# Attention then mixture of experts: one more head turns its score tiles by VectorE and DRAM instead of on TensorE

## The chip, the cores and the metric

The kernel runs on one core of a Trainium2 chip. The metric is the device time of one execution in microseconds. A change of up to 0.3% (2.3 us) is about what a measurement of this kernel cannot tell from no change.

## The reference

There are two stages. The first is attention with a hash mask over 2 batches of 8 heads, 768 tokens and 64 dimensions. The second is a layer of 4 experts on the attention's output. Cut to what matters:

```python
q_bucket, k_bucket = hash6(q @ proj), hash6(k @ proj)      # 6 sign bits
scores = where(q_bucket == k_bucket, q @ k.T / 8, -1e9)
attn = softmax(scores) ; x = attn @ v                      # per batch and head
x = x.transpose -> (1536, 512) ; p = domain_probs / sum
out = sum_e p[:, e] * (relu(x @ w1[e]) @ w2[e])            # w1 512x1024, w2 1024x512
```

All arithmetic has float32 accuracy. The kernel gets it from float32r matmuls, in which each operand is split into a high part and a low part (`...hi`, `...lo`).

## The kernel before

Attention goes through 96 score tiles of 128 queries by 768 keys. There are six tiles to a head, and two neighbouring tiles make a group g, so a head has three groups. A step `i` issues one stage of several tiles. The letters of `ORDER = "THXVSEYNRP"` say which stages stand in a step and in which order. A stage with a lag works on tile `i - lag`. So the row of instructions on each engine is written out by hand, and every engine takes its row strictly in order.

- S (`stage_s`, L344 to L351): TensorE makes the scores of a tile, VectorE takes them out to a tile `p`. E (L367): ScalarE takes the exponential, one step later.
- The `p` tiles must then be turned so that keys lie on partitions. **A heavy head** does this in T (`stage_t`, lag 6): six TensorE transposes of 128x128 (L407), then ScalarE copies them to `pthi` (L411) and VectorE subtracts for `ptlo` (L412).
- **A light head** does it by group. In X (lag 3) VectorE makes two 32x32 block transposes of 128x768 (L426) into `t1`, and SyncE writes `t1` to DRAM (`scr`, L430, 768 KB). In Y (lag 4) SyncE reads it back in four DMAs (L439) into `ptlo`. In H (lag 6) ScalarE copies it in two pieces to `pthi` (L452), and GpSimd subtracts in two pieces (L453).
- V (`stage_v`, L463, lags 7 and 8): TensorE multiplies with the values, first with `pthi`, a step later with `ptlo`. ScalarE and VectorE take out the result (L483, L488 or L495). After an odd head of batch 0 GpSimd scales it and splits it (L497, L501, L504) into the tiles `xs`, the input of the experts.
- P prepares the next head: transposes of q and k (L260), ScalarE (L264) and VectorE (L265), then L276, L278, L284 and five small copies by DMA (L268 to L270, L277, L292).

`LIGHT_FROM` is the number of the first light head (heads are numbered through both batches, 8 is the first head of batch 1).

Up to about 150 us attention of batch 0 runs alone. Then the experts' layer of batch 0 (`moe`) runs on TensorE. Each of 8 units `u` has 8 chunks of 12 matmuls (L683 to L685) with a relu by ScalarE (L690) and a split by VectorE (L691), and then 6 chunks of the second layer (L646 to L648, L652). Attention of batch 1 is put between the chunks: before the next attention stage is issued, a sum of nominal stage costs is compared with the sum of the chunks' costs:

```python
n_att = sum(1306 + 654 * (not light(b, h)) for b, h, t in seq if b) + H * 1632 + LAG_VL * DRAIN
while da < dm * ATT_PACE * n_att / n_moe:   # dm: chunks issued, da: attention issued
```

The last part, the experts' layer of batch 1 (`moe_fast`), starts when all attention is over.

All DMAs are issued from SyncE's queue, also in a fixed order. The experts' weights come in halves of 512 KB (`ws`, L604) into two buffers. VectorE copies one to `w...hi` (L622), GpSimd subtracts for `w...lo` (L615), and only after that is the buffer free for the next `ws`. `PSUM` results use six slots in turn: two large ones, and four small ones that the chunks, T and V share.

In this text tile 48 is the first tile of the first head of batch 1, and its groups are g0 (tiles 48 and 49), g1 and g2. S(54) is the stage S of tile 54.

Of the kernel before, what the change touches and what calls it, by code (L numbers as in the profile page):

```python
# [35 lines left out]
W_STEP = 12  # L36
PREP_AT = 0
ORDER = "THXVSEYNRP"
LIGHT_FROM = 9
LAG_VL = 7  # L40
DRAIN = 1000
LAG_X = 3
# [5 lines left out]
def tile_lsh_attention__then__domain_moe(  # L48
# [276 lines left out]
    def light(b, h):  # L325
        return b * H + h >= LIGHT_FROM

# [634 lines left out]
```

## Time and profile before

| | |
|---|---|
| time, median of 3 runs (lowest, highest) | 753.21 us (751.62, 753.64) |
| span of the profiled execution, first to last instruction | 749.5 us |
| TensorE busy | 733.6 us, 98% of the span |
| VectorE, ScalarE, GpSimd busy | 69%, 48%, 46% |
| TensorE's share of the chain that ended last | 82% |
| TensorE's time in L407 (324 transposes) | 45.8 us as the sum of their lengths |

How to read it: the time of the profiled execution is not listed apart from its span. The median of the runs lies 3.7 us above that span, so that much is taken to lie around it. Matmuls overlap in a pipeline, so what one costs TensorE is the distance between starts, not its listed length. The granted clock of TensorE is a share of 2.4 GHz, 0.5 being the lower level of 1.2 GHz.

### The profile page before, as it was taken

Reading aid. Unit: us, or ns where it says so; the run is one execution under the profiler, and the core shown is the slowest. Engines: PE = TensorE matmul, PEld = TensorE weight load, DVE = VectorE, ACT = ScalarE, POOL = GpSimd, SP = SyncE. Lnnn points to the kernel's source line nnn. Section 1 sums busy time; section 2 is a strip of 40 time slices with the busy share of each in tenths; the row PEclk is TensorE's granted clock in tenths of the full one; section 3 lists DMA queues with packets and bytes.
Section 4 is the critical chain, followed back from the end, with each engine's and each line's share of the span. In section 5 each row is a group of like instructions: output and inputs, shape, how many; then the busy total and the mean of one; then the engine's idle time right before and its main releaser. Section 6 shows DMA issues by size and latency. Waiting matters only on the chain.

```text
span 749.5 us, 11443 instructions
## 1 busy us (share of the span) xinstructions
PE 733.6 (98%) x4090; PEld 668.7 (89%) x4090; DVE 517.3 (69%) x957; ACT 363.2 (48%) x731; POOL 342.7 (46%) x290
## 2 busy tenths in 40 slices
PE   7899999999999999999999999999999999999997
PEld 6798899898998999989999899888988989889896
DVE  4899999856568756686676543887558575675752
ACT  4999999843353544534635210443425234253330
POOL 1233525422466656584857653854334243343430
PEclk9999999999999999999999999999999999999999
DMA  3554454341877697878677511152121221212202
GB/s 99 126 145 102 114 145 122 98 126 61 233 210 195 197 261 224 209 204 247 180 228 225 156 57 57 56 169 85 35 78 57 80 90 30 83 57 68 101 1 84
DMA packets 71953, 95.49 MB, mean 127 GB/s; under 512 B 31396, under 2 KB 47268, under 8 KB 71896
## 3 DMA queue, kind: packets, MB, share of 16 engines
q1 hardware_dynamic: 71896, 94.76, 44.3%
q8 instruction: 32, 0.52, 0.3%
q14 instruction: 25, 0.20, 0.1%
HBM read 62.68 MB, written 19.71 MB: 110 GB/s over the span
## 4 chain that ended last, share of the span: by engine, by line
PE 82%; DVE 8%; ACT 3%; POOL 3%; DMA 2%; issue 1%; SPq 0%; POOLq 0%; DVEq 0%; ACTq 0%
PE mps L646 11%; PE mps L648 11%; PE mps L647 11%; PE mps L683 6%; PE mps L685 6%; PE mps L684 6%; PE pv L463 6%; PE sps L346 3%; PE sps L344 2%; PE mps L841 2%; PE mps L837 2%; PE mps L840 2%; DVE p L351 2%; PE hps L276 2%; PE pa L840 2%; PE pa L837 1%
## 5 line engine op out<-in xcount | busy, mean ns | idle before, releaser
L646 PE MATMUL mps<-w2hi,hh 128*128 128x512 f32 x384 | 151.6, 395 | 0.8 <-DVE acc L654 0.4
L648 PE MATMUL mps<-w2hi,hl 128*128 128x512 f32 x384 | 151.0, 393 | 0.0
L647 PE MATMUL mps<-w2lo,hh 128*128 128x512 f32 x384 | 150.0, 391 | 0.0
L453 POOL TENSOR_TENSOR ptlo<-ptlo,pthi 128x768 fp32r<-128x768 f32 x42 | 78.1, 1880 | 70.1 <-ACT pthi L452 56.1
L654 DVE SCALAR_TENSOR_TENSOR acc<-mps,pe,acc 128x512 f32<-128x512 f32 x84 | 62.7, 747 | 62.0 <-PE mps L648 60.9
L690 ACT ACTIVATE hh<-mps 128x384 fp32r<-128x384 f32 x64 | 31.4, 491 | 139.4 <-PE mps L685 139.2
L823 POOL TENSOR_TENSOR w2lo<-ws,w2hi 128x512 fp32r<-128x512 f32 x32 | 45.9, 1453 | 113.9 <-ACT w2hi L822 113.9
L367 ACT ACTIVATE p<-p,nb 128x768 f32<-128x768 f32 x96 | 89.6, 933 | 11.5 <-DVE p L351 10.7
L351 DVE TENSOR_SCALAR_CACHE_REDUCE p<-sps 128x768 f32<-128x768 f32 x96 | 90.6, 945 | 5.2 <-PE sps L346 4.9
L646 PEld LDWEIGHTS mps<-w2hi,hh 128*128 128x128 f32 x384 | 72.1, 188 | 17.8 <-ACT hh L851 2.8
L648 PEld LDWEIGHTS mps<-w2hi,hl 128*128 128x128 f32 x384 | 72.1, 188 | 17.5 <-DVE hl L852 2.4
L683 PE MATMUL mps<-xs,w1hi 128*128 128x384 f32 x256 | 86.7, 338 | 0.5 <-DVE hl L691 0.5
L685 PE MATMUL mps<-xs,w1lo 128*128 128x384 f32 x256 | 86.2, 337 | 0.0
L684 PE MATMUL mps<-xs,w1hi 128*128 128x384 f32 x256 | 86.0, 336 | 0.0
L647 PEld LDWEIGHTS mps<-w2lo,hh 128*128 128x128 f32 x384 | 72.3, 188 | 13.2
L691 DVE SCALAR_TENSOR_TENSOR hl<-mps,hh 128x384 fp32r<-128x384 f32 x64 | 35.5, 555 | 55.6 <-ACT hh L690 55.0
L615 POOL TENSOR_TENSOR w1lo<-ws,w1hi 128x512 fp32r<-128x512 f32 x32 | 42.0, 1319 | 40.0 <-DVE w1hi L622 38.3
L412 DVE TENSOR_TENSOR ptlo<-ptps,pthi 128x384 fp32r<-128x384 f32 x108 | 54.5, 546 | 7.5 <-ACT pthi L411 7.3
L346 PE MATMUL sps<-k,al 76*128 76x384 f32 x192 | 50.5, 343 | 3.3 <-POOL vv L305 1.7
L344 PE MATMUL sps<-ah,q 128*128 128x384 f32 x192 | 50.6, 344 | 1.9 <-DVE ah L244 1.1
L782 POOL TENSOR_TENSOR w1lo<-ws,w1hi 128x512 fp32r<-128x512 f32 x24 | 35.9, 1496 | 34.0 <-ACT w1hi L778 34.0
L615 POOL TENSOR_TENSOR w2lo<-ws,w2hi 128x512 fp32r<-128x512 f32 x32 | 41.8, 1313 | 20.7 <-issue 6.6
(134 smaller groups left out, 1576.6 us busy)
## 6 DMA issues: line engine op xcount, KB each, us to landing
ws<-in_moe_w_dram SPq DMA_DIRECT2D x64, 512.0 KB
scr<-t SPq DMA_DIRECT2D x21, 768.0 KB
ptlo<-scr SPq DMA_DIRECT2D x84, 192.0 KB
q<-ah SPq DMA_DIRECT2D x30, 192.0 KB
tv<-in_v_dram SPq DMA_DIRECT2D x16, 192.0 KB
rdb<-row SPq DMA_DIRECT2D x48, 64.0 KB
out_dram<-acc SPq DMA_DIRECT2D x12, 256.0 KB
tqk<-in_q_dram SPq DMA_DIRECT2D x15, 192.0 KB
```

Source lines behind the costliest of these rows:

```text
L344: nc.tensor.matmul(ps[:, i, :NH], q1[:, sl], k1[:, i * NH : (i + 1) * NH], start=True, stop=False)
L346: nc.tensor.matmul(ps[:, i, :NH], q2[0:MQE, sl], k2[0:MQE, i * NH : (i + 1) * NH], start=False, stop=True)
L351: nc.vector.tensor_scalar(out=two(pt), in0=ps[:, :, :NH], scalar1=MASKED, scalar2=MASKED, op0=ALU.min, op1=ALU.min, accum_out=nb,)
L367: nc.scalar.activation(pt, pt, ACTF.Exp, bias=nb, scale=-1.0, accum_out=dens[b, h, g][:, o : o + 1])
L453: nc.gpsimd.tensor_tensor(out=fl[:, sl], in0=px[:, sl], in1=fh[:, sl].bitcast(F32), op=ALU.subtract)
L615: nc.gpsimd.tensor_tensor(out=lo[:, c - 1], in0=st[c - 1], in1=hi[:, c - 1].bitcast(F32), op=ALU.subtract)
L646: nc.tensor.matmul(ps, hh[:, ts], w2hi[:, f], start=f == 0, stop=False)
L647: nc.tensor.matmul(ps, hh[:, ts], w2lo[:, f], start=False, stop=False)
L648: nc.tensor.matmul(ps, hl[:, ts], w2hi[:, f], start=False, stop=f == FC - 1)
L683: nc.tensor.matmul(ps[:, :SB], w1hi[:, kk, fs], xhi[b, kk][:, sl], start=kk == 0, stop=False)
L684: nc.tensor.matmul(ps[:, :SB], w1hi[:, kk, fs], xlo[b, kk][:, sl], start=False, stop=False)
L685: nc.tensor.matmul(ps[:, :SB], w1lo[:, kk, fs], xhi[b, kk][:, sl], start=False, stop=kk == KD - 1)
```

## The change

One number changes. Head 8, the first of batch 1, becomes a light head, so its six tiles go through X, Y and H instead of T.

```diff
--- before.py
+++ after.py
@@ -36,7 +36,7 @@
 W_STEP = 12
 PREP_AT = 0
 ORDER = "THXVSEYNRP"
-LIGHT_FROM = 9
+LIGHT_FROM = 8
 LAG_VL = 7
 DRAIN = 1000
 LAG_X = 3
```

`light(b, h)` is `b * H + h >= LIGHT_FROM`. The sum `n_att` falls from 86668 to 82744, and the six costs of 654 that T had returned are no longer counted. Since every stage has a lag of its own, the rows of all engines change from step 52 on. Three places:

ScalarE, where attention of batch 0 ends and the first chunks of the experts begin (the first L690). Before:

```order
L264 ACTIVATE ah<-tps,qk_scale 128x768
L411 ACTIVATE pthi<-ptps 128x3x128 x2
L483 ACTIVATE xtmp<-pv 64x256
L690 ACTIVATE hh<-mps 128x384
L367 ACTIVATE p,den<-p,nb 128x768
L278 ACTIVATE k_2378<-hps,sgn_bias 44x768
L690 ACTIVATE hh<-mps 128x384 x2
```

ScalarE at the same place, now:

```order
L264 ACTIVATE ah<-tps,qk_scale 128x768
L452 ACTIVATE pthi<-ptlo 128x768 x2
L483 ACTIVATE xtmp<-pv 64x256
L690 ACTIVATE hh<-mps 128x384
L367 ACTIVATE p,den<-p,nb 128x768
L278 ACTIVATE k_2380<-hps,sgn_bias 44x768
L690 ACTIVATE hh<-mps 128x384 x4
L367 ACTIVATE p,den<-p,nb 128x768
L370 ACTIVATE den<-den,eps 128x2
L452 ACTIVATE pthi<-ptlo 128x768 x2
```

The two copies of g0, which wait for its four DMAs, now stand ahead of the first relu of the experts; those of g1 stand behind the fifth relu.

GpSimd at the same place (`xs_120` is the last of the four input tiles of the experts, `ws` the second half of `w2` of unit 0). Before:

```order
L504 TENSOR_TENSOR xs_120<-xf,xs_120 128x256
L615 TENSOR_TENSOR w2lo<-ws,w2hi 128x512
L497 TENSOR_TENSOR xf<-xf,rdb 128x256
L501 TENSOR_SCALAR xs_120<-xf 128x256
L504 TENSOR_TENSOR xs_120<-xf,xs_120 128x256
L615 TENSOR_TENSOR w2lo<-ws,w2hi 128x512
```

GpSimd now:

```order
L504 TENSOR_TENSOR xs_120<-xf,xs_120 128x256
L453 TENSOR_TENSOR ptlo<-ptlo,pthi 128x768 x2
L497 TENSOR_TENSOR xf<-xf,rdb 128x256
L501 TENSOR_SCALAR xs_120<-xf 128x256
L504 TENSOR_TENSOR xs_120<-xf,xs_120 128x256
L615 TENSOR_TENSOR w2lo<-ws,w2hi 128x512 x2
L453 TENSOR_TENSOR ptlo<-ptlo,pthi 128x768 x2
```

Both L615 that read the weights' buffer now stand behind the subtractions of g0.

SyncE's queue from the last small copy of head 8 on (`k_2127`). Before:

```order
L292 DMA k_2127<-al 12x768
L383 DMA row<-rt 4x32 x2
L190 DMA tv<-in_v_dram 128x384
L390 DMA rdb<-row 64x256
L383 DMA row<-rt 4x32 x2
L268 DMA q_2375<-ah 64x768
L269 DMA q_2375<-ah 64x768
L270 DMA k_2378<-ah 64x768
L604 DMA ws<-in_moe_w_dram 128x2x512 x2
L390 DMA rdb<-row 64x256
```

SyncE's queue now, from the write of g0 that stands behind the same `k_2127`:

```order
L430 DMA scr<-t_2275 128x1536
L383 DMA row<-rt 4x32 x2
L190 DMA tv<-in_v_dram 128x384
L439 DMA ptlo<-scr 32x4x384 x4
L390 DMA rdb<-row 64x256
L430 DMA scr<-t_2349 128x1536
L383 DMA row<-rt 4x32 x2
L268 DMA q_2377<-ah 64x768
L269 DMA q_2377<-ah 64x768
L270 DMA k_2380<-ah 64x768
L604 DMA ws<-in_moe_w_dram 128x2x512 x2
L439 DMA ptlo<-scr 32x4x384 x4
```

The four DMAs that read g1 back stand behind the two `ws`. The second of these needs the buffer that the two L615 read. On TensorE the first L463 of g0 stood behind four chunks and one T; it now stands behind three chunks, and the first L463 of g1 behind six.

## Rows read from the trace of the kernel before

**Rows 1.** Windows: window, its length, each engine's busy us (count), PEclk, DMA share, GB/s.
```profile
200.00:250.00 50.00, 50.00 (x282) 46.97 (x282) 31.36 (x58) 23.25 (x44) 26.74 (x21) 1.00 0.81 225
```

**Rows 2.** Timeline of TensorE: start us, length, engine, line, tiles, [idle before <-releaser].
```profile
142.54 0.55 PE L407 MATMUL ptps<-ident,p 128*128 128x128 f32 x3 [0.37 <-DVE ptlo L412]
...
147.67 0.59 PE L346 MATMUL sps<-k,al 76*128 76x384 f32 x2 [1.24 <-POOL xf L497]
...
150.13 0.34 PE L683 MATMUL mps<-xs,w1hi 128*128 128x384 f32 x1
...
152.21 0.51 PE L344 MATMUL sps<-ah,q 128*128 128x384 f32 x2
...
153.97 0.33 PE L683 MATMUL mps<-xs,w1hi 128*128 128x384 f32 x1
...
158.13 0.82 PE L407 MATMUL ptps<-ident,p 128*128 128x128 f32 x6
...
158.71 0.42 PE L683 MATMUL mps<-xs,w1hi 128*128 128x384 f32 x1
...
160.90 0.88 PE L463 MATMUL pv<-pthi,vv 128*128 128x256 f32 x6
...
162.32 0.34 PE L683 MATMUL mps<-xs,w1hi 128*128 128x384 f32 x1
...
164.44 0.82 PE L407 MATMUL ptps<-ident,p 128*128 128x128 f32 x6
...
165.77 0.44 PE L683 MATMUL mps<-xs,w1hi 128*128 128x384 f32 x1 [0.52 <-DVE hl L691]
...
181.18 0.82 PE L407 MATMUL ptps<-ident,p 128*128 128x128 f32 x6
...
182.19 0.50 PE L646 MATMUL mps<-w2hi,hh 128*128 128x512 f32 x1 [0.19 <-DVE acc L652]
```

**Rows 3.** Timeline of VectorE, the first of the existing transposes.
```profile
178.22 1.83 DVE L426 STREAM_TRANSPOSE t<-p 128x768 f32<-128x768 f32 x2
```

**Rows 4.** Timeline of SyncE's queue: start us, length of issuing, line, tiles, count.
```profile
145.21 0.78 SPq L292 DMA_DIRECT2D k<-al  x1
...
180.07 0.35 SPq L430 DMA_DIRECT2D scr<-t  x1
...
212.32 0.39 SPq L604 DMA_DIRECT2D ws<-in_moe_w_dram  x1
...
272.89 2.86 SPq L439 DMA_DIRECT2D ptlo<-scr  x4
...
367.37 1.80 SPq L439 DMA_DIRECT2D ptlo<-scr  x4
```

**Rows 5.** Windows of half a microsecond, columns as in the first group.
```profile
182.50:183.00 0.50, 0.50 (x4) 0.38 (x3) 0.47 (x3) 0.08 (x1) 0.46 (x1) 1.00 0.51 197
...
218.50:219.00 0.50, 0.50 (x5) 0.50 (x4) 0.50 (x2) 0.00 (x0) 0.42 (x2) 1.00 0.22 41
```

**Rows 6.** Timeline of ScalarE, three of the 21 existing groups' copies.
```profile
195.03 1.57 ACT L452 ACTIVATE pthi<-ptlo 128x768 fp32r<-128x768 f32 x2
...
280.69 1.58 ACT L452 ACTIVATE pthi<-ptlo 128x768 fp32r<-128x768 f32 x2 [2.71 <-DMA ptlo<-scr]
...
372.78 1.58 ACT L452 ACTIVATE pthi<-ptlo 128x768 fp32r<-128x768 f32 x2 [1.00 <-DMA ptlo<-scr]
```

**Rows 7.** Timeline of GpSimd.
```profile
152.78 0.74 POOL L497 TENSOR_TENSOR xf<-xf,rdb 128x256 f32<-128x256 f32 x1 [2.67 <-DVE xf L495]
...
154.79 1.28 POOL L615 TENSOR_TENSOR w2lo<-ws,w2hi 128x512 fp32r<-128x512 f32 x1
...
195.95 3.66 POOL L453 TENSOR_TENSOR ptlo<-ptlo,pthi 128x768 fp32r<-128x768 f32 x2 [4.08 <-ACT pthi L452]
```

**Rows 8.** Windows early in the span, columns as in the first group.
```profile
14.00:18.00 4.00, 3.53 (x11) 3.15 (x12) 1.36 (x4) 1.49 (x4) 0.00 (x0) 0.57 0.59 148
...
22.00:23.00 1.00, 0.00 (x0) 0.00 (x0) 0.41 (x3) 0.98 (x5) 0.63 (x1) 1.00 0.21 37
```

## The prediction

> **What bounds the kernel now.** I read the page's busy shares first, then the windows by stage. Then TensorE is busy all the time: in the stretch from 200 to 250 us it works 50.00 of 50 us at the full clock, while VectorE, ScalarE and GpSimd work half of it or a little more and the DMA engines 0.81 [rows 1]. So a TensorE instruction taken out there is worth its distance to the next start, and nothing given to another engine costs anything until TensorE waits for it. The first thing to see in the timeline of TensorE is that the change lies in two different stretches. Ahead of 150 us attention runs alone and S(54) waits until 147.67; behind 150.13 the experts' chunks run [rows 2]. The row of that wait names GpSimd's L497, but what L346 reads is `k2`, whose last piece the small copy of L292 brings, issued at 145.21 [rows 4].
>
> **What goes.** Six T. The T of tiles 48 and 49 lie ahead of 150 us. The first is hidden by S(54), which goes on at 147.67 with it or without it; the second I count at nothing, because VectorE is later there (below). The T of tiles 50 to 53 lie between chunks: 0.58 us from 158.13 to 158.71; 1.33 from 164.44 to 165.77, with a wait of 0.52 for VectorE behind it; 0.58 for tile 52 like the first; 1.01 from 181.18 to 182.19, with a wait of 0.19 [rows 2]. Sum: **3.5 us less**. ScalarE and VectorE lose their copies and subtractions of these tiles; they bound nothing here.
>
> **What comes.** For each of three groups: two VectorE transposes, 1.83 us together [rows 3], a write of 768 KB, four reads, two ScalarE copies of 1.57 together [rows 6], two GpSimd subtractions of 3.66 together [rows 7]. The 21 existing groups do the same, and TensorE stays full. But their copies wait for DMA beside work that has slack; the first groups of head 8 come where the engines pass from attention to the experts, and the rows of instructions show what stands behind them. So I walk along them.
>
> Write of g0. The buffer `t1` that it takes holds tiles 46 and 47, so VectorE waits for the T of tile 47, over at 142.54 + 0.55 = 143.1 [rows 2], and is done at 144.9 by the 1.83. SyncE is busy with the small copy ahead of it until 145.21 + 0.78 = 146.0 [rows 4], and issues the write then. The small copy goes first, so S(54) still starts its second half at 147.67. I take 150.1 for the first chunk as before; bounds are 0.58 earlier (the T that is gone) and 1.8 later (if all VectorE transposes were on the path).
>
> Reads of g0. The first existing write was issued at 180.07, and its traffic ended in the window from 182.50, half busy, so at 182.8 [rows 4, 5]. With 0.3 us to be noticed, an estimate, that is 3.0 us from issue to landing; the reads are issued at 149.0. Four reads took 5.4 us from issue to the copy that waited for them (367.37 to 372.78), at worst 7.8 (272.89 to 280.69, with other copies around) [rows 4, 6]. I take 5.4, since the queue is nearly empty here: ScalarE's copies of g0 start at 154.4. Until then ScalarE stands still, and behind it wait the taking out of the last V of batch 0 and all relus. That alone costs TensorE nothing: it has three chunks to do first.
>
> The second half of `w1`. It takes the buffer that both L615 read. They stand behind the subtractions of g0 and the last three L497 to L504. From the start of the copies: 0.92 until GpSimd starts (195.03 to 195.95), 3.66, 2.01 (152.78 to 154.79), and twice 1.28 [rows 6, 7], 9.15 in all. So SyncE issues this load at 163.6; before, the second L615 was over at 154.79 + 1.28 = 156.1 [rows 7]. SyncE is in order, and **behind the load stand the four reads of g1**, whose own write had landed long ago.
>
> Reads of g1. A load of 512 KB and four reads behind it in a quiet queue were issued from 212.32 on, and their traffic ended at about 218.7 [rows 4, 5], 6.4 us; the copy notices some half a microsecond later (estimate from the above), and two head loads now follow in the queue, so I take 7.0 (6.4 to 8.3, the latter 0.5 for the load's issue and the 7.8). The copies of g1 start at 170.6 and end at 172.2.
>
> TensorE needs both copies for the first V of g1, which stands behind six chunks (2.08 each, 150.13 to 152.21), three S, two V and one L276: 1.76 for S and L276 (152.21 to 153.97), twice 1.42 for V and S (160.90 to 162.32) [rows 2]. 150.1 + 12.5 + 1.8 + 2.8 = 167.2. So **TensorE waits 5.0 us**, with nothing else to do since it is in order too. The third group has time: its write follows at about 171, its reads land some 8.4 us (3.0 + 5.4) behind that, and its first V stands four chunks, two S and two V later.
>
> The clock. The only low clock of the trace stands early: 0.57 on average over the 4 us from 14 us on, after a stretch with waits, which cost (1 - 0.57) x 4 = 1.7 us of full speed; but a window of 1 us without any matmul passed at the full clock [rows 8]. Five microseconds of nothing are nearer to the first, so I add **1.7**; the other bound is 0. The Trainium skill ("TensorE: Matmul & The Clock Gate", section "HAM oscillation — how this bites in real kernels") tells of waits for DMA that send the array back to its lower clock each time. By that rule the 1.7 is to be paid; by the row of 22 us alone nothing, and the sum would be 1.7 lower. No wait of this trace is long enough to show which.
>
> **Sum**: -3.5 + 5.0 + 1.7 = +3.2 us. Made on the profiled execution (749.5 span, 3.7 around it by the median), it goes onto the median: 753.2 + 3.2 = **756.4 us**. Bounds: -0.6 (6.4 instead of 7.0) and -1.7 (no lower clock) give 754.1, and the earlier start of 0.58 does not help, since the wait then grows by as much. Upwards 2.4 (7.8 for the reads of g0) and 1.3 (8.3 for those of g1) give 760.1.
>
> **The rivals.**
> The clock holds. All else as above: +1.5, 754.7, no change that can be measured. For it speaks the window without matmuls at 22 us, against it that the wait is five times as long.
>
> The DMAs are faster, and TensorE does not wait: faster than before. The two round trips lie in a queue with little else. If the reads ran at the write's pace, 2.1 us or so instead of 4, both trips would save about 4 us, the wait would shrink to 1.0, too short to move the clock, and the time would be 753.2 - 2.5 = 750.7. It decides once the copies of g1 land 3.8 us sooner than I worked out (then 1.2 of wait against 3.5). Against it: the reads of 367.37 and those behind the load of 212.32 had little beside them either, and took their 5.4 and 6.4.
>
> The DMAs are slower, as in the rows of 272.89: the upper bound, 760.1. Then the first V of g0 waits too. For it: the write of g1 is issued while the reads of g0 still run.
>
> Waits later on: the attention stages of batch 1 stand at other places beside the chunks, and the pace is 4.5% lower by `n_att`. ScalarE's wait for reads of up to 2.71 in the rows shown stayed without a wait of TensorE; I count nothing.
>
> **How the numbers follow.** The walk with both terms: 0.46, 755.5 to 758.5. Clock holds: 0.25, 754 to 755.4. DMAs faster: 0.12, 749.7 to 751. Slower, or a wait more: 0.17, 758.5 to 762. The range of 8 in 10 reaches from 750.6 to 759.9 and leaves out about half of the last case and of the faster one. Slower by over 0.3% (above 755.5) are the first and the last case and little of the second: 0.60. Within 0.3%: 0.28. Faster: 0.12.
>
> **What would show it.** In the new profile: the first two L452 at about 154.4, with ScalarE idle for some 3 us ahead of them; the load behind them issued at about 163.6, at once after the second L615; a wait of TensorE of about 5 us before an L463 near 167, released by ScalarE's L452; a window behind it with a granted clock near 0.5; no wait of TensorE over a microsecond from there to the end of attention; and four T fewer between chunks. The prediction is wrong if the reads of g1 are issued well before 163, if TensorE has work there that I did not see, or if later waits outweigh this one.

## The result, and the profile after

The changed kernel takes 756.66 us (median of 4 runs, 755.20 to 757.16), the kernel before 752.63 beside it: 1.0055 times as long, interval 1.0042 to 1.0067, so 4.0 us slower. A second comparison gave 756.44 against 751.85, 1.0064 (1.0052 to 1.0077). The prediction was 756.4, slower.

The waits of TensorE in the profile after (total, count, longest) begin with one that is new; the longest of all others is 1.4 us:

```profile
PE pv L463 <- ACT pthi L452: 5.5, 1, 5.5
```

The timeline of TensorE around it (before: [rows 2]), with S(54), L260, the first chunk, S(55), the first V of g0 and both V of g1:

```profile
146.68 0.59 PE L344 MATMUL sps<-ah,q 128*128 128x384 f32 x2 [0.69 <-issue]
148.44 0.98 PE L346 MATMUL sps<-k,al 76*128 76x384 f32 x2 [1.17 <-DMA k<-al]
149.32 1.54 PE L260 MATMUL tps<-ident,tqk 128*128 128x128 f32 x6
...
151.85 0.34 PE L683 MATMUL mps<-xs,w1hi 128*128 128x384 f32 x1
...
153.94 0.51 PE L344 MATMUL sps<-ah,q 128*128 128x384 f32 x2
...
159.86 0.88 PE L463 MATMUL pv<-pthi,vv 128*128 128x256 f32 x6
...
174.67 1.65 PE L463 MATMUL pv<-pthi,vv 128*128 128x256 f32 x6 [5.46 <-ACT pthi L452]
...
182.37 0.88 PE L463 MATMUL pv<-ptlo,vv 128*128 128x256 f32 x6
```

The first V of g0 waits for nothing; the first V of g1 waits 5.46 us, from 169.21 on. To see why, read SyncE's queue, GpSimd and ScalarE in turn [rows 4, 7, 6]:

```profile
146.88 0.46 SPq L430 DMA_DIRECT2D scr<-t  x1
...
150.31 1.76 SPq L439 DMA_DIRECT2D ptlo<-scr  x4
...
152.72 0.58 SPq L430 DMA_DIRECT2D scr<-t  x1
...
157.36 8.36 SPq L604 DMA_DIRECT2D ws<-in_moe_w_dram  x2
165.82 1.84 SPq L439 DMA_DIRECT2D ptlo<-scr  x4
```

```profile
156.96 3.83 POOL L453 TENSOR_TENSOR ptlo<-ptlo,pthi 128x768 fp32r<-128x768 f32 x2 [6.58 <-ACT pthi L452]
160.75 0.74 POOL L497 TENSOR_TENSOR xf<-xf,rdb 128x256 f32<-128x256 f32 x1
...
162.76 2.54 POOL L615 TENSOR_TENSOR w2lo<-ws,w2hi 128x512 fp32r<-128x512 f32 x2
```

```profile
156.03 1.58 ACT L452 ACTIVATE pthi<-ptlo 128x768 fp32r<-128x768 f32 x2 [4.23 <-DMA ptlo<-scr]
...
173.04 1.58 ACT L452 ACTIVATE pthi<-ptlo 128x768 fp32r<-128x768 f32 x2 [5.46 <-DMA ptlo<-scr]
```

The two issues of `ws` span 8.36 us together, although one takes 0.39 elsewhere [rows 4]. The second goes out when the second L615 is over, at 162.76 + 2.54 = 165.3. The four reads of g1 stand right behind, at 165.82, while their write had been issued at 152.72. The copies of g1 start at 173.04, and V starts as they end.

The granted clock is the column ahead of the last two in the windows:

```profile
146.00:148.00 2.00, 0.59 (x2) 0.30 (x2) 1.93 (x7) 1.03 (x2) 1.53 (x2) 1.00 0.22 65
148.00:149.00 1.00, 0.56 (x2) 0.50 (x2) 0.97 (x2) 0.00 (x0) 0.66 (x1) 0.66 0.95 399
149.00:150.00 1.00, 1.00 (x5) 0.68 (x4) 0.97 (x3) 0.70 (x1) 0.83 (x3) 0.50 0.76 296
150.00:151.00 1.00, 1.00 (x7) 1.00 (x6) 1.00 (x2) 0.73 (x4) 0.38 (x1) 0.50 0.61 143
...
170.00:172.00 2.00, 0.00 (x0) 0.00 (x0) 0.00 (x0) 0.00 (x0) 0.00 (x0) 1.00 1.11 228
172.00:174.00 2.00, 0.00 (x0) 0.00 (x0) 0.00 (x0) 0.96 (x2) 0.04 (x1) 0.55 1.26 206
174.00:176.00 2.00, 1.33 (x6) 1.33 (x7) 0.94 (x2) 1.95 (x4) 2.00 (x2) 0.50 1.15 373
176.00:178.00 2.00, 2.00 (x8) 2.00 (x8) 2.00 (x5) 0.45 (x2) 1.89 (x2) 0.50 0.17 69
178.00:180.00 2.00, 2.00 (x10) 2.00 (x10) 0.56 (x1) 0.25 (x1) 1.83 (x3) 0.74 0.92 227
```

It is low twice: behind the wait, as forecast, and already from 148 on, which the prediction did not see.

A second trace of the same kernel, taken for experiment 7, shows S(55), the wait and both V of g1 at:

```profile
154.04 0.51 PE L344 MATMUL sps<-ah,q 128*128 128x384 f32 x2
...
174.06 1.65 PE L463 MATMUL pv<-pthi,vv 128*128 128x256 f32 x6 [4.76 <-ACT pthi L452]
...
182.35 0.88 PE L463 MATMUL pv<-ptlo,vv 128*128 128x256 f32 x6
```

**A measure without the start.** The program's first 140 us vary: S(53), which no edit but `W_STEP` moves, starts at 143.64 in the trace of before and between 143.99 and 145.75 in the others, mostly by waits in the first 60 us. So I also give, for each trace, the stretch from the start of S(53) to the end of the span. The time of a run is 1.7 to 1.8 us above its span.

| kernel | S(53) | span | from S(53) on | against before |
|---|---|---|---|---|
| before | 143.64 | 749.5 | 605.86 | |
| after, two traces | 144.40, 143.99 | 755.0, 755.0 | 610.60, 611.01 | +4.7, +5.2 |
| reads ahead, two traces | 145.75, 144.65 | 749.5, 748.3 | 603.75, 603.65 | -2.1, -2.2 |
| wait filled | 144.74 | 753.5 | 608.76 | +2.9 |
| 148 filled | 144.61 | 755.7 | 611.09 | +5.2 |
| weights early | 145.12 | 749.3 | 604.18 | -1.7 |
| reads ahead and 148 filled, two traces | 144.27, 144.83 | 747.2, 748.3 | 602.93, 603.47 | -2.9, -2.4 |
| before with W_STEP = 10 | 145.68 | 750.5 | 604.82 | -1.0 |
| last group alone | 144.94 | 749.2 | 604.26 | -1.6 |

### The profile page after: what moved, and what is told of

The parts are those of the page before. It is cut to its first block, busy times and chain, and to the rows that moved or that the text cites. A ratio compares the mean times of both kernels' runs of the same rounds, so it can differ in the third digit from the quotient of the medians.

```text
span 755.0 us, 11408 instructions
## 1 busy us (share of the span) xinstructions
PE 733.9 (97%) x4054; PEld 668.1 (88%) x4054; DVE 521.7 (69%) x951; ACT 364.0 (48%) x725; POOL 352.9 (47%) x296
## 4 chain that ended last, share of the span: by engine, by line
PE 81%; DVE 10%; DMA 4%; POOL 3%; issue 1%; ACT 1%; SPq 1%; POOLq 0%; DVEq 0%; ACTq 0%
PE mps L646 11%; PE mps L648 11%; PE mps L647 11%; PE pv L463 6%; PE mps L683 5%; PE mps L685 5%; PE mps L684 5%; DVE p L351 3%; PE sps L346 3%; PE sps L344 3%; PE mps L841 2%; PE mps L837 2%; PE mps L840 2%; PE hps L276 2%; PE ptps L407 2%; DVE ptlo L412 2%
## 5 line engine op out<-in xcount | busy, mean ns | idle before, releaser
L453 POOL TENSOR_TENSOR ptlo<-ptlo,pthi 128x768 fp32r<-128x768 f32 x48 | 89.2, 1880 | 77.5 <-ACT pthi L452 70.3
L690 ACT ACTIVATE hh<-mps 128x384 fp32r<-128x384 f32 x64 | 31.3, 491 | 119.4 <-PE mps L685 119.2
L615 POOL TENSOR_TENSOR w2lo<-ws,w2hi 128x512 fp32r<-128x512 f32 x32 | 41.9, 1317 | 31.5 <-DVE w2hi L622 23.2
L412 DVE TENSOR_TENSOR ptlo<-ptps,pthi 128x384 fp32r<-128x384 f32 x96 | 48.4, 545 | 6.0 <-ACT pthi L411 5.8
L452 ACT ACTIVATE pthi<-ptlo 128x768 fp32r<-128x768 f32 x48 | 37.8, 836 | 30.5 <-DMA ptlo<-scr 30.4
L615 POOL TENSOR_TENSOR w1lo<-ws,w1hi 128x512 fp32r<-128x512 f32 x32 | 41.6, 1306 | 22.7 <-DVE w1hi L622 16.9
```

Of the source, the lines that this page charges most:

```text
L453: nc.gpsimd.tensor_tensor(out=fl[:, sl], in0=px[:, sl], in1=fh[:, sl].bitcast(F32), op=ALU.subtract)
L615: nc.gpsimd.tensor_tensor(out=lo[:, c - 1], in0=st[c - 1], in1=hi[:, c - 1].bitcast(F32), op=ALU.subtract)
```

## The experiments

**1. The reads of g1 ahead of the held load.** The second half of `w1` is issued behind them; no other instruction moves.

```diff
 def load_w():
+    if cursor[0] == 5 and not held:
+        held.append(1)
+        return
 ...
 def stage_y(b, h, g):
     ...
     pxs[b, h, g] = (px, lo)
+    if (b, h, g) == (1, 0, 1):
+        load_w()
```

> The kernel after, with one move in SyncE's queue: the four reads of g1 are issued ahead of the second half of w1 instead of behind it. Nothing else moves. Theory (the load that is held until 165.3 holds the reads behind it): the reads go out at about 158 instead of 165.8 and land at 163.5 to 165, TensorE comes to the first V of g1 at 169.2 and finds it ready; the wait of 5.5 us and the low clock behind it (about 2.0) go, so 756.7 - 7.5 = 749.2. Rival A (the round trip through DRAM is itself too long here, with its write, the other load and the neighbours in the queues): the copies still end behind 169.2, a wait of 2 to 5 us stays, 752 to 757. Rival C (the wait only moves, to the first V of g2 or to the weights of the next unit, whose second half is now issued behind the reads): no wait at g1, one of similar size later, 754 to 757.

Measured: 749.93 us (6 runs), 0.9968 of before (0.9956 to 0.9979). SyncE's queue (the edit moves line numbers: L610 is L604, L440 is L439):

```profile
158.47 1.17 SPq L610 DMA_DIRECT2D ws<-in_moe_w_dram  x1
160.94 1.74 SPq L440 DMA_DIRECT2D ptlo<-scr  x4
166.77 0.40 SPq L610 DMA_DIRECT2D ws<-in_moe_w_dram  x1
```

TensorE, the first V of g1 (here L466):

```profile
170.66 0.34 PE L691 MATMUL mps<-xs,w1lo 128*128 128x384 f32 x1
171.13 0.98 PE L466 MATMUL pv<-pthi,vv 128*128 128x256 f32 x6
```

ScalarE, the copies of g1 (here L455):

```profile
169.50 1.58 ACT L455 ACTIVATE pthi<-ptlo 128x768 fp32r<-128x768 f32 x2
```

The load is held as long as in after (it goes out 21.0 us behind S(53), in after 20.9), but the reads of g1 no longer stand behind it. V starts as ScalarE's copies end, at 171.08; it stands 0.47 us behind the last matmul of the chunk, where matmuls of a chunk stand 0.17 apart, so what is left of the wait is 0.3 us. The whole loss is gone, and 2.1 to 2.4 us of the 3.5 for the T that were taken out show. The theory holds, though the time is 0.7 us above the 749.2 expected; the round trip is short enough, and behind 150 us the longest wait listed is 0.4 us. A third buffer for `ws`, which would free the load itself, was not tried.

**2. The wait filled.** In stage V of g1, ahead of its first matmul:

```diff
     ps = pvs[b, h, g]
+    if (b, h, g, part) == (1, 0, 1, 0):
+        for _ in range(50):
+            nc.tensor.transpose(ps[:, :P], ident, ident)
```

> The kernel after, with 50 transposes of the identity put into TensorE's row directly ahead of the first V of g1, into the PSUM tile that this V then overwrites. At 0.58 us for six they last 4.8 us, so they fit into the wait of 5.5 and should change nothing but what TensorE does in it. Theory (the clock falls because TensorE stands still): the granted clock stays at 1.00 from 169 to 179, the wait in front of V shrinks to about 0.6, V starts at the same 174.7, and the stretch behind it costs 2.0 less: 754.7. Rival B (the clock's fall has another cause, or the four windows at 0.5 cost nothing that the end feels): 756.7 as after, with the low clock as before or without it.

Measured: 755.34 us, 1.0037 of before (1.0024 to 1.0051), so 1.3 us less than after; each taken against the kernel before beside it, 1.0 to 1.5 less.

```profile
175.22 0.96 PE L466 MATMUL pv<-pthi,vv 128*128 128x256 f32 x6
...
180.94 0.88 PE L466 MATMUL pv<-ptlo,vv 128*128 128x256 f32 x6
```

```profile
170.00:172.00 2.00, 2.00 (x21) 2.00 (x19) 0.00 (x0) 0.00 (x0) 0.00 (x0) 1.00 1.12 227
172.00:174.00 2.00, 2.00 (x21) 2.00 (x20) 0.00 (x0) 0.54 (x1) 0.00 (x0) 1.00 1.22 185
174.00:176.00 2.00, 2.00 (x20) 2.00 (x19) 0.52 (x2) 1.95 (x5) 1.62 (x1) 1.00 1.23 296
```

The clock stays at 1.00. From the first V of g1 to its second part it takes 5.72 us (175.22 to 180.94) where after took 7.70 (174.67 to 182.37): the low clock cost 1.98 us, as expected. In the second trace of after it took 8.29 (174.06 to 182.35), so 2.57 us more. The 50 transposes took 5.38 us instead of 4.8 and start V a little late, and the start of the program differs by 0.3; from S(53) on the kernel is 1.8 and 2.3 us shorter than the two traces of after (table).

**3. The stretch at 148 filled.** Two times six transposes of the identity, in stage V of batch 0's last group and ahead of L260 of head 10, as far as TensorE goes in place of T(48) and T(49):

```diff
+    if (b, h, g, part) == (0, 7, 2, 0):
+        for _ in range(6):
+            nc.tensor.transpose(ps[:, :P], ident, ident)
 ...
     ps = big("tps")
+    for _ in range(6 * ((b, h) == (1, 2))):
+        nc.tensor.transpose(ps[:, 0, NH:512], ident, ident)
```

> The kernel after, with two times six transposes of the identity at the places at which the T of tiles 48 and 49 stood (ahead of the first V of batch 0's last group, and ahead of L260). The granted clock from 148 to 152 should go back to 1.00 and the first chunk start 1 us sooner. Theory (the end of the wait is set by SyncE's chain of reads, relayed by ScalarE and GpSimd, and by nothing that TensorE does there): the wait at the first V of g1 grows from 5.5 to about 6.4 and the time stays, 756.7. Rival (the low clock at 148 is part of the loss by itself): 755.7, with the wait as long as before.

Measured: 757.41 us, 1.0068 (1.0055 to 1.0080).

```profile
150.00:152.00 2.00, 2.00 (x19) 2.00 (x18) 2.00 (x3) 1.74 (x4) 0.60 (x1) 1.00 0.54 128
```

SyncE's reads of g0 (here L441), and both V of g1 (here L468):

```profile
150.51 2.98 SPq L441 DMA_DIRECT2D ptlo<-scr  x4
```

```profile
175.77 1.65 PE L468 MATMUL pv<-pthi,vv 128*128 128x256 f32 x6 [6.68 <-ACT pthi L454]
...
183.03 0.88 PE L468 MATMUL pv<-ptlo,vv 128*128 128x256 f32 x6
```

The clock at 148 stays up, the first chunk starts at 151.62 and S(55) 9.09 us behind S(53) (after: 9.54), and the wait grows from 5.46 to 6.68. TensorE's own gain of 0.45 went into the wait whole. The wait grew by more than the gain because the chain ended later: V starts 31.16 us behind S(53), in after 30.27. Half of that is there at the copies of g0, whose four reads took 2.98 to issue instead of 1.76. They took 2.76 to 2.98 in all three traces with these transposes and 1.76 in the five others in which they stand at the same place in the queue; why is not shown. So the edit also moves the chain, and this run alone does not show that TensorE has no part in its end. The two traces of after show it without an edit: S(55) stands 9.54 and 10.05 us behind S(53), the wait is 5.46 and 4.76, and V starts 30.27 and 30.07 behind S(53). What TensorE loses ahead of the wait only makes the wait shorter.

**4. The weights' splits earlier.** `W_STEP = 10` instead of 12, so both L615 stand ahead of the subtractions of g0.

```diff
-W_STEP = 12
+W_STEP = 10
```

> The kernel after with W_STEP = 10 instead of 12: the splits of unit 0's weights come earlier in attention of batch 0, so both L615 that keep the buffer stand ahead of the subtractions of g0 on GpSimd, and the first of the two loads of the next weights goes out ahead of the write of g0. The second load then stands at the same place in SyncE's queue but is not held. Theory: no issue of several us in SyncE's queue near 157 to 166, the reads of g1 go out at 158 to 159, no wait of TensorE over 1.5 us at the first V of g1: 749 to 750. Rival A (the round trip itself is too long): the load goes out unheld and a wait of 2 us or more stays, 752 to 757. Rival D (the wait comes from GpSimd's row, the subtractions L453 of g0 behind the copies, not from the load): the load is free and the wait is nearly as long, 755 to 757.

Measured: 752.09 us (11 runs), 0.9995 (0.9986 to 1.0003). SyncE's queue and TensorE:

```profile
159.31 0.65 SPq L604 DMA_DIRECT2D ws<-in_moe_w_dram  x1
160.99 1.74 SPq L439 DMA_DIRECT2D ptlo<-scr  x4
```

```profile
150.05 0.88 PE L260 MATMUL tps<-ident,tqk 128*128 128x128 f32 x6 [1.44 <-DVE p L351]
...
170.97 0.99 PE L463 MATMUL pv<-pthi,vv 128*128 128x256 f32 x6
```

The load is not held and the wait is gone, which breaks the same chain at another link. But the time is 2 us worse than expected. From S(53) on the kernel is within 0.5 us of the one with the reads ahead (table), so most of it, some 1.7 us, was lost ahead of S(53).

**5. Control: before with the same step.**

> The kernel before with W_STEP = 10, the control of the run with the weights' splits earlier, which lost its wait and still ended 2.2 us behind the run with the reads moved. Theory (the earlier splits cost about 2 us by themselves in attention of batch 0, where VectorE is nearly full, and have nothing to do with head 8): 752.3 + 2 = 754.3. Rival (what that run lost, it lost in head 8's groups, by the load ahead of the write of g0 and the second load behind): 752.3, no change.

Measured: 752.21 us, 1.0005 (0.9996 to 1.0014). My theory of 2 us for the whole kernel is wrong. The rival's time was met, but not its reason, since experiment 4 lost little in head 8's groups. The table shows it: 1.0 us faster from S(53) on and no faster in all, so the step costs 1 us or somewhat more ahead of S(53). Before gets it back, because S(54) no longer waits for `k` (1.24 us, [rows 2]). With head 8 light TensorE can't: the wait for `k` is gone there as well, but VectorE has its two block transposes in its row, and L260 waits 1.44 us for it, as shown above: it stands 4.93 us behind S(53), as in experiment 1.

**6. The last group alone.** Only tiles 52 and 53 are turned by VectorE and DRAM; `light` takes the tile as well.

```diff
-def light(b, h):
-    return b * H + h >= LIGHT_FROM
+def light(b, h, t=0):
+    return (b * H + h) * NT + t >= LIGHT_FROM * NT + 4
```

> One part of the change alone: only the last group of head 8 (tiles 52 and 53) is turned by VectorE and DRAM, tiles 48 to 51 by TensorE as before. Nothing of a round trip then lies ahead of the two halves of w1. Theory (each T between chunks is worth its distance, 0.58 and 1.01, and the loss came from g0 and g1 alone): 752.3 - 1.6 = 750.7, no wait over 1 us at the V of this group, the clock at 1.00 from 145 to 200. Rival (the first group that comes back from DRAM stalls TensorE wherever it stands): a wait of 2 to 5 us at its first V and no gain, 752 to 756. Rival (a T is hidden and worth nothing): 752.3.

Measured: 750.16 us, 0.9978 (0.9969 to 0.9987), and -1.6 in the table: the price of these two T (0.58 + 1.01). So a first group from DRAM does not stall TensorE wherever it stands. This one's reads went out at 170.18, long after the two loads of `w1` (over at 157.8), and 15.8 us ahead of its V:

```profile
186.00 0.88 PE L463 MATMUL pv<-pthi,vv 128*128 128x256 f32 x6
```

**7. The reads ahead and the stretch at 148 filled.** The edits of 1 and 3 together.

> Both edits at once: the reads of g1 ahead of the second half of w1, and two times six transposes of the identity at the places of the T of tiles 48 and 49. With the wait gone, TensorE's own time there should count again. From S(53) to S(55) TensorE took 8.57 us before, 9.98 with the reads moved alone and 9.09 with the transposes alone. Theory (first six T less, then the low clock at 150 to 154 given back): 749.9 - 0.9 = 749.0, no wait of TensorE over 1.5 us behind 100 us, no window behind 100 us at a clock below 0.9. Rival (the low clock there is hidden behind the copies of g0 or g1, for which TensorE would wait now): 749.9 as without the transposes.

Measured: 749.53 us, 0.9972 (0.9960 to 0.9983). This is not the expected 0.9 us below experiment 1. So after, experiment 1 and this one were run again side by side:

> The kernel after once more, unchanged, on the same chip as the next two, since the starts of the programs scatter by up to 2 us from execution to execution (S(53) began at 143.64 to 145.75 in the traces so far) and the question of the next two is one of 0.9 us. Expected 4.0 us above before.

> The reads of g1 ahead of the second half of w1, unchanged, once more. Expected 2.4 us below before, ratio 0.9968.

> The same with the twelve transposes at the places of T(48) and T(49), unchanged, once more. In the traces this saves 0.89 us from S(53) to S(55), and from S(55) on the two kernels take the same time. Theory (that saving is in the end's time, and start-up scatter hid it): 0.9 us below the kernel without the transposes, ratio to before about 0.9956. Rival (it is lost again somewhere): the same as without them.

Measured: 756.44, 749.92 (0.9978, 0.9969 to 0.9987) and 749.73 us (0.9975, 0.9966 to 0.9984). The transposes do bring S(55) 0.7 to 0.9 us nearer to S(53) and hold the clock at 1.00, but the medians differ by 0.4 and 0.2 us, less than the intervals, and against the kernel before beside each the first pair even differs the other way (0.9972 with the transposes, 0.9968 without). Of two traces of this kernel one keeps the whole gain to the end (-2.9) and one loses most of it again behind S(55) (-2.4). Whether the fill is worth anything stays open; the order of the reads is what counts. Both kernels are faster than after by 6.5 to 6.7 us, and than before by 0.2 to 0.3%: all four intervals lie below 1, though a change of this size is near what one comparison can tell.

## Why the prediction was right

**The four T between chunks, -3.5.** Experiment 6 gives two of them their price. With the reads ahead, the traces from S(53) on are -2.1 and -2.2; adding back what S(53) to S(55) lost (9.98 and 9.78 us instead of 8.57) leaves -3.5 and -3.4.

**The chain, +5.0.** Right link by link, each to within 0.8 us. The times of after, less the 0.76 by which its S(53) is late, with the forecast in brackets: write at 146.1 (146.0), reads of g0 at 149.6 (149.0), copies at 155.3 (154.4), the load at 164.5 (163.6), copies of g1 at 172.3 (170.6), their end and V at 173.9 (172.2). From the copies of g0 to the load it took 9.27 us (9.15), from the load to the copies of g1 7.7 (7.0): the chain ended 1.7 us later than forecast, nearly half of it in the last four reads. Another 0.4 lies between the write of g0 and its reads, 3.43 us instead of 3.0; the 0.3 in it for being noticed, an estimate, rested on no row. TensorE arrived at 168.5 (167.2), 1.3 later, so the wait grew by only 0.46. Experiments 1 and 4 show the cause by breaking the chain at two links; the two traces of after show that TensorE has no part in its end. The Trainium skill ("DMA: Bandwidth & Descriptors", section "Anatomy of one DMA — SWDGE (gpsimd) path") says of GpSimd's path that a DMA's wait happens on the issuing sequencer, ahead of dispatch; the trace shows the same for SyncE's queue, where the held load kept the ready reads of g1 behind it until 165.82.

**The clock, +1.7.** 1.98 by experiment 2, which also shows that standing still is what lowered it here: with TensorE busy and all else waiting, it stays at 1.00. The size varies from trace to trace: 2.57 in the second of after, 1.54 in experiment 3 (7.26 us between the two V instead of 5.72). The Trainium skill ("TensorE: Matmul & The Clock Gate", section "HAM oscillation — how this bites in real kernels") tells of such a price behind waits for DMA; the trace agrees, with 0.50 in the windows from 174 to 178.

**The first chunk at an unchanged time, 0.** This step was wrong, within its bounds: from S(53) to S(55) it took 9.54 us instead of 8.57, 0.97 more. Three things make this up. First VectorE, with the block transposes in its row, is later, and L260 waits for it. The rows of before, and that of experiment 1, in which the wait is listed:

```profile
148.10 0.82 PE L260 MATMUL tps<-ident,tqk 128*128 128x128 f32 x6
148.75 0.82 PE L407 MATMUL ptps<-ident,p 128*128 128x128 f32 x6
149.33 0.96 PE L463 MATMUL pv<-ptlo,vv 128*128 128x256 f32 x6
```

```profile
150.68 0.88 PE L260 MATMUL tps<-ident,tqk 128*128 128x128 f32 x6 [0.32 <-DVE p L351]
```

L260 stands 4.46 us behind S(53) in before, 4.92 in after and 4.93 in experiment 1: 0.46 more. Second, T(49) is gone, 0.58 less (148.75 to 149.33). These two all but cancel, so the prediction's nothing for this T was right, and for its reason. Third, what it did not see: the clock fell at 148 (0.50 to 0.66 until 152). From L260 to S(55) before took 4.11 with T(49) in it, so 3.53 without, and after 4.62: 1.09 more. In the second trace of after it was 1.59. In the changed kernel all this costs nothing of its own, since an earlier arrival only makes the wait longer (the two traces of after); 0.97 and 5.46 together are the one term that was forecast as 5.0. It costs something once the wait is gone: experiment 1 keeps 2.1 to 2.2 of the 3.5.

**The sum.** -3.5 + 0.97 + 5.46 + 1.98 = 4.9, against 4.7 in the table for this trace and 3.2 as forecast. In the second trace it is -3.5 + 1.48 + 4.76 + 2.57 = 5.3, against 5.2. What was too small is the chain's end (1.7, less the 0.3 that chunks and stages took longer ahead of the wait), and the clock by 0.3. The medians say 4.0 and 4.6. That the time was met so closely is luck: the forecast met the first measured time to 0.3 us because it went onto a median of 753.2 that was 0.6 and 1.4 us above the two measured beside the changed kernel. What I took to lie around the span, 3.7 us, is 1.7: the profiled execution of before was a quick one. The sum does not rest on it.

**Rivals.** Clock holds: no. Faster DMAs: no, the round trips were slower than I took. Slower DMAs: only in part; the reads took 5.7 us instead of 5.4 and 7.7 instead of 7.0, short of the bounds of 7.8 and 8.3, and the first V of g0 waited for nothing. Waits later on: none; the kernels with the reads ahead keep what they gain. The chances of the two cases above 755.5 add up to 0.63, not to 0.60.

## What to carry to other kernels

In a queue that is worked off in order a transfer that must wait for a buffer delays every transfer behind it, ready or not; here that was 6 us for the reads of g1. Before a stage gets a round trip through DRAM, walk its DMAs along the queue and put those that are ready ahead of those that are held. A wait of TensorE costs more than its length when its clock falls in it, here 1.5 to 2.6 us on top of 4.8 to 6.7. And before trusting a gain of 0.1%, measure from an instruction that the change cannot move to the end, since the start of a program scatters more than that.

## What was not expected of the hardware

The granted clock fell without a long stop. After, TensorE worked 0.59 of the 2 us from 146 on, with gaps of 0.69 and 1.17 us, and the clock was at 0.50 to 0.66 from 148 to 152; with the twelve transposes of the identity it worked 1.44 of these 2 us, had the same gap of 1.15 us for `k`, and the clock stayed at 1.00. The second stretch came after TensorE had stopped at 169.21: the window of 170 to 172 shows 1.00, those from 172 to 178 0.50 to 0.55, that of 178 to 180 0.74, although work had begun again at 174.67.
